# First batch of a banded attention and feed-forward kernel: band windows of v loaded first, the feed-forward cut at f = 4 and 9, other staging places for the weights

## The chip, the cores and the metric

The kernel runs on one core of a Trainium2 chip. The metric is the device time of one execution in microseconds (us), as the median of several runs. The engines are TensorE (PE, with its weight loads PEld), VectorE (DVE), ScalarE (ACT), GpSimd (POOL) and SyncE (SP). In this kernel SP only issues the transfers.

## The reference, cut to what matters

```python
# q, k, v: (8 batches, 8 heads, 576 positions, 64)
q_d, k_d, v_d = mean over 4 neighbouring positions          # 144 positions
out_up    = repeat(softmax(q_d k_d^T / 8) v_d, 4)            # the pooled part
out_local = softmax(q k^T / 8 where |i - j| < 4) v           # the banded part
x   = out_up + out_local, as (8 * 576 tokens, 512)
h   = x @ w_in                                               # (512, 2048)
out = max(0.01 * h, h) @ w_out                               # (2048, 512)
```

Everything is float32. The weights are float64 in memory (two 32-bit words per number).

## The kernel before, in words

**The feed-forward (called MoE in the names).** A half of a batch is a tile of 256 tokens (hf = 0) or 320 tokens (hf = 1). The hidden dimension is cut into 16 blocks f of 128. One step (half, f) is 12 matmuls of the up projection (L638), two activations and a subtraction (`leaky`, L648 to L651), and 12 matmuls of the down projection (L678) into four accumulators, the PSUM banks `acc0` to `acc3`. Each float32 product is made of three matmuls, on a high and a low part: `xh`, `xl` of x, `wih`, `wil`, `woh`, `wol` of the weights, `gh`, `gl` of the activation. `PASSES` lists the halves with their range of f. For batch 0 each half is done in two ranges, f 0 to 7 and f 8 to 15, in the order (0,0) low, (0,1) low, (0,0) high, (0,1) high. What a first range leaves is stored to the output (`store`, ACT copy at L713), loaded again (`refetch`) and added to the second range (DVE, L704). The other batches take all 16 blocks at once.

**The weights.** `convert(f, k)` brings one tile of w_in (k = 0) or w_out (k = 1): it takes a staging place, loads 512 KB, and makes the high and low parts with ACT (L226, L231, L239), DVE (L228, L233) and POOL (L241). There are 32 such tiles. The staging place is a buffer of another stage: `k`, `v`, the two `prod`, `up`, and for f below 4 also `xh1` and `xl1`. It is held until the POOL instruction at L241 is done. For f of 9 and above there is room for the result only when the pool `su` is closed (signal `late`), after all pooled and banded work of batch 0.

**Batch 0.** For each pair of heads c (four of them), `pooled(0, c)` makes the pooled attention (scores L312, softmax with ACT L324, transposes L351, values L363). `banded(0, c, hf)` makes the banded part with small matmuls: a mask and scores (L405, L413), the softmax (DVE L420, L421, L426, L430, ACT L424, L428, POOL L432), transposes (L440) that ACT copies into `su_pt` (L442), then the values (L458) from `su_pt` and the band windows of v, `su_vw`, and at last the sum with the pooled part and the split into `xh` and `xl` (L470, L475, L477). `su_pt` has two buffers, so two (c, hf) are under way at a time. `su_vw` has four. The load of a window is asked for only after the transposes, inside `banded`. The second half waits until all four c of the first half have their x.

**The other batches.** `scores` and `values` make the band with POOL products (L507, L562) and DVE sums (L513, L568), `widen` spreads the pooled part into `up`, `landing` transposes and adds (L598, L605, L611, L613). `pooled` needs `qk` and `vs`, one buffer each.

**The order.** All of it is written by a planner (`Order`): each task is a generator with a rank; the next instruction is the one that can start first by the planner's costs, and among equal ones that of the lowest rank. The engines, and SP with its transfers, then run their instructions strictly in the planned order. Buffers are granted to the waiting task of the lowest rank.

Of the kernel before, what the change touches and what calls it, by code (L numbers as in the profile page):

```python
# [6 lines left out]
F32 = mybir.dt.float32  # L7
# [25 lines left out]
WORDS = 2  # L33
REBIAS = 2.0 ** -112
LOW, ROUND = 0.876 * 2.0 ** -29, 0.484375
HF = NF // 2
PASSES = ([((0, 0), 0, HF), ((0, 1), 0, HF), ((0, 0), HF, NF), ((0, 1), HF, NF)]
# [107 lines left out]
def attn_moe(ctx: ExitStack, tc, qkt, vd, qb, kb, vb0, vb1, vwb, band, identb, w_in, w_out, ident, edge, out):  # L145
# [8 lines left out]
                xloc=2, lst=3, lvw=1, gh=3, gl=3, o=4, hp=2, pt=2, xh0=1, xl0=1, xh1=1, xl1=1, acc0=1, acc1=1, acc2=1, acc3=1,  # L154
                su_vw=NC, su_pt=2)
# [20 lines left out]
    def pe(us, *after):  # L176
        return (yield ("op", "PE", us, max(after) + SAFE, 0))
# [38 lines left out]
    def convert(f, k):  # L216
        s = yield from slot("k", "v", "prod", "up", *(("xh1", "xl1") if f < 4 else ()))
# [38 lines left out]
    def x_tile(b, hf):  # L256
        if b:
            yield from wait(("xbuf", b - 1, hf))
        elif hf:
            yield from wait(("x", 0, 0), NC)  # L260
# [4 lines left out]
        t = yield from wait(("done", b, hf), 2 if b == 0 else 1)  # L265
# [3 lines left out]
    def fetch(b, c, pool):  # L269
# [3 lines left out]
        else:  # L273
            sq = sv = None
            qk = pool.tile([128, 2, S], F32, name=f"qk{c}")
            vs = pool.tile([72, 2, 2, D, FAC], F32, name=f"vs{c}")
# [96 lines left out]

    shared, wide = {}, {}
# [4 lines left out]
    def banded(b, c, hf, rank, pool=None):  # L379
# [7 lines left out]
        if b:  # L387
            yield from wait("late")
        elif hf:
            yield from wait(("x", 0, 0), 4)  # L390
# [10 lines left out]
        s_b = yield from slot("hp" if (b, hf) == (0, 0) else "pt")  # L401
# [43 lines left out]
        if b:  # L445
            yield from wait(("pooled", b, NC - 1))
            yield from wait(("xbuf", b, hf))
        s_vw = yield from (slot("su_vw") if b == 0 else slot("q", "lvw"))
        vw = sb(s_vw, [WIN, 5, 2, D], F32, pool)
        tv = yield from load(vw[:, :nb], vwb[b, c, :, b0:b1], 35840 * nb, s_vw.t)  # L450
# [125 lines left out]
    def widen(b, hf, u):  # L576
        to = yield from wait(("pooled", b, 2 * u))
        to = max(to, (yield from wait(("pooled", b, 2 * u + 1))))
        tx = yield from wait(("xbuf", b, hf))
        s_u = yield from slot("up")  # L580
# [41 lines left out]
    def up_proj():  # L622
        for i, (p, f) in enumerate(steps):
# [3 lines left out]
            if f == f0:  # L627
                tx = yield from wait(("x", b, hf), 4)
            tw = yield from wait(("w", f, 0))
# [26 lines left out]
    def down_proj():  # L656
        for i, (p, f) in enumerate(steps):
# [5 lines left out]
            if f == f0 + 2 and f0 > 0:  # L663
# [26 lines left out]
    def refetch(p, e, n):  # L690
        s_o = yield from slot("o")
        o = sb(s_o, [128, 320], F32)
        tw = yield from wait(("half", PASSES[p][0]), 4)
# [4 lines left out]
    def store(p, e, n, s_a, acc, t):  # L698
# [18 lines left out]
        if f1 < NF:  # L717
            od.signal(("half", key), t)
# [11 lines left out]
    with tc.manual_schedule():  # L730
# [5 lines left out]
        for c in range(NC):  # L736
            od.spawn(1 + c, pooled(0, c, 1 + c, sup))
            od.spawn(1.5 + c, banded(0, c, 0, 1.5 + c, sup))
            od.spawn(26 + 0.1 * c, banded(0, c, 1, 26, sup))
        for f in range(NF):  # L740
            for k in range(2):
                od.spawn((20 if f < HF else 40) + 2 * (f % HF) + k, convert(f, k))
# [74 lines left out]
```

## Time and profile before

| | |
|---|---|
| median of 3 runs | 985.31 us (983.8 to 986.4) |
| profiled execution | 980.87 us, span 979.1 us, mean granted clock 0.983 |
| PE busy, matmuls | 948.0 us (97%), 7434 |
| DVE busy | 616.5 us (63%) |
| ACT busy | 432.2 us (44%) |
| POOL busy | 613.5 us (63%) |
| moved by DMA | 106.46 MB, mean 109 GB/s |

Busy time is a sum over the whole span. Matmuls are pipelined, so their single durations overlap. In a timeline row the columns are start, duration, engine, line, operation, output and inputs, shape, count, and in brackets the idle time before it with what ended it. In a row by windows the columns are the window, its length, the busy time of each engine with its count of instructions, the granted TensorE clock, the share of DMA time and GB/s.

### The profile page before, as it was taken

To read this page: it belongs to the slowest core of one execution; us is meant where nothing else is said; L and a number is where in the kernel's file an instruction comes from. 1 tells how busy PE (TensorE), PEld (TensorE's weight loads), DVE (VectorE), ACT (ScalarE), POOL (GpSimd) and SP (SyncE) were. 2 spreads that over 40 slices of the span, in tenths; PEclk is the share of its full clock that TensorE was granted. 3 is DMA by queue.
4 is the path that set the end of the run, shared out by engine and by line. 5 is a ranking of instruction groups with operands and counts; after the bars stand their busy time and mean duration, and the time that the engine had idled before them with its cause. 6 is when DMAs were issued, how large, how long until landed. Compare 5 with 4: busy or idle time off the path is not lost.

```text
span 979.1 us, 18709 instructions
## 1 busy us (share of the span) xinstructions
PE 948.0 (97%) x7434; PEld 913.0 (93%) x7434; DVE 616.5 (63%) x987; ACT 432.2 (44%) x1251; POOL 613.5 (63%) x362
## 2 busy tenths in 40 slices
PE   5796999999999999999999999999999999999998
PEld 4596999889999999999999999999999999999998
DVE  4997778878866877587665976547563756151111
ACT  4887966444533543255422554234332324242212
POOL 3553467888797878887787878758695777310000
PEclk9597999999999999999999999999999999999999
DMA  9546763624531542225223441304131121000000
GB/s 286 188 148 204 232 223 127 197 99 156 166 108 56 185 136 94 68 92 179 82 89 109 154 147 61 111 4 158 39 108 55 54 71 52 30 23 6 23 1 27
DMA packets 51959, 106.46 MB, mean 109 GB/s; under 512 B 4464, under 2 KB 30320, under 8 KB 51872
## 3 DMA queue, kind: packets, MB, share of 16 engines
q1 hardware_dynamic: 51872, 105.28, 32.9%
q8 instruction: 58, 0.95, 0.4%
q14 instruction: 29, 0.24, 0.1%
HBM read 94.64 MB, written 10.62 MB: 108 GB/s over the span
## 4 chain that ended last, share of the span: by engine, by line
PE 91%; DMA 3%; ACT 2%; issue 1%; DVE 1%; POOL 1%; SPq 0%; POOLq 0%; ACTq 0%
PE hp L638 42%; PE acc L678 40%; PE pt L312 2%; PE pt L363 2%; PE pt L351 2%; DMA su_vw<-in_vwb_dram 1%; PE pt L598 1%; DMA v<-in_w_out_dram 1%; DMA vs<-in_vd_dram 1%; POOL wol L241 0%; POOL wil L241 0%; DVE prod L228 0%; PE pt L413 0%; ACT pd L324 0%; SPq L181 0%
## 5 line engine op out<-in xcount | busy, mean ns | idle before, releaser
L562 POOL TENSOR_TENSOR prod<-v,s 128x896 f32<-128x896 f32 (+1 forms) x112 | 270.1, 2417 | 85.8 <-DVE xloc L568 64.3
L638 PE MATMUL hp<-xh,wih 128*128 128x320 f32 (+1 forms) x1024 | 312.7, 305 | 1.7 <-ACT xh L611 1.3
L678 PE MATMUL acc<-gh,woh 128*128 128x320 f32 (+1 forms) x1024 | 307.9, 301 | 0.5 <-ACT o L713 0.4
L638 PE MATMUL hp<-xl,wih 128*128 128x320 f32 (+1 forms) x1024 | 304.0, 297 | 0.1
L638 PE MATMUL hp<-xh,wil 128*128 128x320 f32 (+1 forms) x1024 | 303.8, 297 | 0.0
L678 PE MATMUL acc<-gh,wol 128*128 128x320 f32 (+1 forms) x1024 | 301.8, 295 | 0.0
L678 PE MATMUL acc<-gl,woh 128*128 128x320 f32 (+1 forms) x1024 | 301.7, 295 | 0.0
L507 POOL TENSOR_TENSOR prod<-q,k 128x896 f32<-128x896 f32 (+1 forms) x112 | 265.1, 2373 | 36.1 <-DMA k<-in_kb_dram 22.9
L648 ACT ACTIVATE gh<-hp 128x320 fp32r<-128x320 f32 (+1 forms) x256 | 105.4, 412 | 364.5 <-PE acc L678 339.6
L651 DVE TENSOR_TENSOR gl<-hp,gh 128x320 fp32r<-128x320 f32 (+1 forms) x256 | 116.2, 455 | 221.4 <-ACT hp L649 220.3
L638 PEld LDWEIGHTS hp<-xh,wih 128*128 128x128 f32 x1024 | 194.6, 190 | 8.6 <-issue 5.5
L678 PEld LDWEIGHTS acc<-gh,woh 128*128 128x128 f32 x1024 | 192.7, 188 | 4.7 <-issue 2.6
L638 PEld LDWEIGHTS hp<-xl,wih 128*128 128x128 f32 x1024 | 195.0, 190 | 0.3 <-DVE xl L613 0.3
L638 PEld LDWEIGHTS hp<-xh,wil 128*128 128x128 f32 x1024 | 194.8, 190 | 0.0
L678 PEld LDWEIGHTS acc<-gl,woh 128*128 128x128 f32 x1024 | 192.7, 188 | 0.0
L678 PEld LDWEIGHTS acc<-gh,wol 128*128 128x128 f32 x1024 | 192.4, 188 | 0.0
L568 DVE TENSOR_REDUCE xloc<-prod 128x128 f32<-128x896 f32 (+1 forms) x112 | 133.9, 1196 | 22.7 <-POOL prod L562 21.4
L513 DVE TENSOR_REDUCE s<-prod 128x14 f32<-128x896 f32 (+1 forms) x112 | 133.4, 1193 | 19.5 <-POOL prod L507 19.1
L649 ACT ACTIVATE hp<-hp 128x320 f32<-128x320 f32 (+1 forms) x256 | 104.0, 406 | 0.0
L605 DVE TENSOR_TENSOR pt<-pt,up 128x256 f32<-128x256 f32 (+1 forms) x56 | 38.7, 709 | 32.3 <-PE pt L598 30.6
L299 DVE TENSOR_REDUCE qk_d<-qk 128x288 f32<-128x1152 f32 x29 | 38.9, 1342 | 11.8 <-DMA qk<-in_qkt_dram 11.7
L324 ACT ACTIVATE pd<-pt,st_d 128x144 f32<-128x144 f32 x84 | 32.0, 381 | 26.8 <-DVE st_d L321 19.5
(119 smaller groups left out, 777.5 us busy)
## 6 DMA issues: line engine op xcount, KB each, us to landing
qk<-in_qkt_dram SPq DMA_DIRECT2D x32, 576.0 KB
k<-in_kb_dram SPq DMA_DIRECT2D x14, 704.0 KB
v<-in_vb_dram SPq DMA_DIRECT2D x14, 704.0 KB
vs<-in_vd_dram SPq DMA_DIRECT2D x32, 288.0 KB
k<-in_kb_dram SPq DMA_DIRECT2D x14, 640.0 KB
v<-in_vb_dram SPq DMA_DIRECT2D x14, 640.0 KB
out_dram<-o SPq DMA_DIRECT2D x36, 160.0 KB
out_dram<-o SPq DMA_DIRECT2D x36, 128.0 KB
```

The source lines that it names most:

```text
L299: nc.vector.tensor_reduce(out=qk_d, in_=qkr, axis=AX.X, op=ALU.add)
L324: nc.scalar.activation(out=pd[:, qi], in_=scv[:, qi], func=AF.Exp, scale=SCALE / (FAC * FAC), bias=mx[:, qi:qi + 1], accum_out=sm[:, qi:qi ...
L507: nc.gpsimd.tensor_tensor(out=prv, in0=q[:, p, a - j0:z - j0].unsqueeze(2).to_broadcast([128, n, W, D]), in1=view(k[:, p], (a - j0) * D, [ ...
L513: nc.vector.tensor_reduce(out=s[:, p, a - j0:z - j0], in_=prv, axis=AX.X, op=ALU.add)
L562: nc.gpsimd.tensor_tensor(out=prv, in0=view(v[:, p], a - j0, [[1, n], [nv, D], [1, W]]), in1=s[:, p, a - j0:z - j0].unsqueeze(2).to_broadc ...
L568: nc.vector.tensor_reduce(out=xl_t[:, :n, p], in_=prv, axis=AX.X, op=ALU.add)
L605: nc.vector.tensor_tensor(out=xv, in0=xv, in1=upv, op=ALU.add)
L638: nc.tensor.matmul(hp[:, :n], wt[:, c], x[:, c], start=k == 0, stop=k == 3 * NC - 1)
L648: nc.scalar.activation(out=gh[:, :n], in_=hp[:, :n], func=AF.Prelu, alpha=0.01)
L649: nc.scalar.activation(out=hp[:, :n], in_=hp[:, :n], func=AF.Prelu, alpha=0.01)
L651: nc.vector.tensor_tensor(out=gl[:, :n], in0=hp[:, :n], in1=gh[:, :n].bitcast(F32), op=ALU.subtract)
L678: nc.tensor.matmul(acc[:, :n], wt[:, es], g[:, :n], start=f == f0 and j == 0, stop=f == f1 - 1 and j == 2)
```

## The change

- `PASSES`: batch 0 is done in three ranges of f, cut at 4 and 9, each range for both halves. So there are two more passes that store what they have, and two more that load it again. `refetch` is asked for one step earlier and waits for the pass two before it.
- The windows of v get tasks of their own (`windows`), with ranks from 1.2 to 8.2. The first half's windows have their four `su_vw` buffers and are no longer asked for after the transposes; the second half's windows use the four buffers of `vs` of batch 0 (`su_vs`) after these have been summed.
- The second half of `banded(0)` and its `xh1`, `xl1` wait for the scores of c = 3 of the first half, not for the whole x; its rank is 21, not 26.
- The score bank of the first half is `acc{(c + 2) % 4}`, not `hp`.
- Staging places: `v`, `up`, `vs` and a new buffer `stg` for all f, in addition `k` and the two `prod` for f below 8, and `xh1`, `xl1` for f below 4. The ranks of `convert` follow f alone.
- The planner's cost of small PE groups rises by 0.09 us; `widen` takes `up` in a fixed order.

```diff
+OWN = 8
-HF = NF // 2
-PASSES = ([((0, 0), 0, HF), ((0, 1), 0, HF), ((0, 0), HF, NF), ((0, 1), HF, NF)]
+CUTS = (0, 4, 9, NF)
+PASSES = ([((0, hf), f0, f1) for f0, f1 in zip(CUTS, CUTS[1:]) for hf in range(2)]
           + [((b, hf), 0, NF) for b in range(1, B) for hf in range(2)])
...
-                xloc=2, lst=3, lvw=1, gh=3, gl=3, o=4, hp=2, pt=2, xh0=1, xl0=1, xh1=1, xl1=1, acc0=1, acc1=1, acc2=1, acc3=1,
-                su_vw=NC, su_pt=2)
+                xloc=2, lst=3, stg=1, gh=3, gl=3, o=4, hp=2, pt=2, xh0=1, xl0=1, xh1=1, xl1=1, acc0=1, acc1=1, acc2=1, acc3=1,
+                su_vw=NC, su_vs=NC, su_pt=2)
...
-        return (yield ("op", "PE", us, max(after) + SAFE, 0))
+        return (yield ("op", "PE", us + 0.09, max(after) + SAFE, 0))
...
     def convert(f, k):
-        s = yield from slot("k", "v", "prod", "up", *(("xh1", "xl1") if f < 4 else ()))
+        s = yield from slot("v", "up", "vs", "stg", *(("k", "prod") if f < OWN else ()), *(("xh1", "xl1") if f < 4 else ()))
...
     def x_tile(b, hf):
...
         elif hf:
-            yield from wait(("x", 0, 0), NC)
+            yield from wait(("scored", 0, NC - 1))
...
-        t = yield from wait(("done", b, hf), 2 if b == 0 else 1)
+        t = yield from wait(("done", b, hf), len(CUTS) - 1 if b == 0 else 1)
...
     def fetch(b, c, pool):
...
-            sq = sv = None
+            sq, sv = None, (yield from slot("su_vs"))
             qk = pool.tile([128, 2, S], F32, name=f"qk{c}")
-            vs = pool.tile([72, 2, 2, D, FAC], F32, name=f"vs{c}")
+            vs = sb(sv, [72, 2, 2, D, FAC], F32, pool)
...
+    vws = {}
+
+    def windows(c, hf, pool):
+        b0, b1 = BLKS[hf]
+        s_vw = yield from slot("su_vs" if hf else "su_vw")
+        vws[c, hf] = s_vw, sb(s_vw, [WIN, 5, 2, D], F32, pool)
+        t = yield from load(vws[c, hf][1][:, :b1 - b0], vwb[0, c, :, b0:b1], 35840 * (b1 - b0), s_vw.t)
+        od.signal(("vw", c, hf), t)
...
     def banded(b, c, hf, rank, pool=None):
...
         elif hf:
-            yield from wait(("x", 0, 0), 4)
+            yield from wait(("scored", 0, NC - 1))
...
-        s_b = yield from slot("hp" if (b, hf) == (0, 0) else "pt")
+        s_b = yield from slot(f"acc{(c + 2) % NC}" if (b, hf) == (0, 0) else "pt")
...
-        if b:
-            yield from wait(("pooled", b, NC - 1))
-            yield from wait(("xbuf", b, hf))
-        s_vw = yield from (slot("su_vw") if b == 0 else slot("q", "lvw"))
-        vw = sb(s_vw, [WIN, 5, 2, D], F32, pool)
-        tv = yield from load(vw[:, :nb], vwb[b, c, :, b0:b1], 35840 * nb, s_vw.t)
+        tv = yield from wait(("vw", c, hf))
+        s_vw, vw = vws[c, hf]
...
     def widen(b, hf, u):
...
+        if (b, hf, u) != (BANDED, 0, 0):
+            yield from wait(("up", *((b, hf, 0) if u else (b, 0, 1) if hf else (b - 1, 1, 1))))
         s_u = yield from slot("up")
...
-            if f == f0 + 2 and f0 > 0:
+            if f == f0 + 1 and f0 > 0:
...
-        tw = yield from wait(("half", PASSES[p][0]), 4)
+        tw = yield from wait(("half", p - 2), 4)
...
-            od.signal(("half", key), t)
+            od.signal(("half", p), t)
...
-            od.spawn(26 + 0.1 * c, banded(0, c, 1, 26, sup))
+            od.spawn(21 + 0.1 * c, banded(0, c, 1, 21, sup))
+            for hf in range(2):
+                od.spawn(1.2 + c + 4 * hf, windows(c, hf, sup))
...
-                od.spawn((20 if f < HF else 40) + 2 * (f % HF) + k, convert(f, k))
+                od.spawn(20 + 2 * f + k, convert(f, k))
```

More of the change, by code (lines that the diff above doesn't have):

```diff
@@ L628, in up_proj @@
                 tx = yield from wait(("x", b, hf), 4)
+                od.signal("started")
             tw = yield from wait(("w", f, 0))
```

## The prediction

> **What bounds the kernel now.** I read the page first, then the span by windows, the chain of waits, and the timelines of PE, ACT, DVE, POOL and SP over the first 200 us.
>
> ```profile
> PE   5796999999999999999999999999999999999998
> PEclk9597999999999999999999999999999999999999
> ```
> ```profile
> 0.00:48.50 48.50, 32.36 (x295) 22.37 (x295) 34.14 (x62) 32.28 (x86) 21.10 (x25) 0.80 0.78 239
> 48.50:77.50 29.00, 28.79 (x291) 27.29 (x289) 26.98 (x52) 25.07 (x64) 15.29 (x12) 0.99 0.52 167
> 77.50:92.90 15.40, 7.67 (x86) 5.89 (x84) 11.45 (x18) 10.59 (x28) 4.05 (x4) 0.80 0.77 243
> 92.90:193.10 100.20, 99.81 (x769) 93.99 (x770) 79.67 (x127) 66.79 (x188) 66.67 (x41) 0.98 0.57 180
> 193.10:199.30 6.20, 3.05 (x26) 2.22 (x25) 5.49 (x14) 3.41 (x13) 2.83 (x2) 1.00 1.02 374
> 199.30:979.10 779.80, 776.27 (x5977) 761.22 (x5977) 458.75 (x718) 294.05 (x876) 503.59 (x280) 1.00 0.25 84
> ```
>
> The page's 40 slices show PE full from the ninth on, so the kernel is PE-bound for 780 of its 979 us and only the first 200 us have anything to give. The windows (first busy time: PE, third: DVE) cut these at the events of PE. To 48.5 us there is no MoE step. To 77.5 us half (0,0) runs f 0 to 7 with PE full: the weights come fast enough. To 92.9 us PE has no MoE step, since x of half (0,1) isn't there. Then it is full to 193.1 us, waits 6.2 us for x of half (1,0), and never again.
>
> ```profile
> 85.51 3.93 DMA su_vw<-in_vwb_dram
> 92.90 4.26 PE hp L638 x15
> 116.64 3.96 PE acc L678 x27
> 199.29 5.24 PE hp L638 x29
> 213.08 2.87 PE hp L638 x24
> ```
>
> These rows of the chain (start, duration, what) give the prices: 0.12 us per matmul of 256 tokens (213.08), 0.147 of 320 (116.64), so a step of 24 costs 2.87 or 3.5 us. They also show that a wait is paid twice: after the wait to 92.9 us 15 matmuls take 4.26 us instead of 2.2, after that to 199.3 us 29 take 5.24 instead of 3.5.
>
> **The change part by part.**
>
> *Windows ahead.* Why is x(0,1) ready only at 93 us?
>
> ```profile
> 16.48 1.28 SPq L181 DMA_DIRECT2D su_vw<-in_vwb_dram  x1
> 73.37 0.38 SPq L181 DMA_DIRECT2D su_vw<-in_vwb_dram  x1
> 133.23 4.53 SPq L181 DMA_DIRECT2D out_dram<-o  x3
> ```
> ```profile
> 19.77 0.24 ACT L442 COPY su_pt<-pt 70x128 f32<-70x128 f32 x1
> 24.23 0.26 ACT L442 COPY su_pt<-pt 70x128 f32<-70x128 f32 x1
> 41.70 0.64 ACT L442 COPY su_pt<-pt 70x384 f32<-70x384 f32 x2 [0.17 <-PE pt L440]
> 59.91 0.37 ACT L442 COPY su_pt<-pt 70x256 f32<-70x256 f32 x1
> ```
> ```profile
> 27.75 0.69 PE L458 MATMUL acc<-su_pt,su_vw 70*64 70x64 f32 x16
> 28.37 0.29 PE L405 MATMUL hp<-band_sb,idb_sb 128*128 128x280 bf16 x1
> 33.00 1.12 PE L458 MATMUL acc<-su_pt,su_vw 70*64 70x64 f32 x16
> 34.06 0.41 PE L405 MATMUL hp<-band_sb,idb_sb 128*128 128x280 bf16 x1
> 43.91 1.12 PE L458 MATMUL acc<-su_pt,su_vw 70*64 70x64 f32 x16 [0.98 <-DMA su_vw<-in_vwb_dram]
> 46.72 0.47 PE L405 MATMUL pt<-band_sb,idb_sb 128*128 128x350 bf16 x1
> 64.80 0.80 PE L458 MATMUL pt<-su_pt,su_vw 70*64 70x64 f32 x20
> 69.47 0.32 PE L405 MATMUL pt<-band_sb,idb_sb 128*128 128x350 bf16 x1
> 89.58 1.34 PE L458 MATMUL pt<-su_pt,su_vw 70*64 70x64 f32 x20 [3.71 <-DMA su_vw<-in_vwb_dram]
> ```
>
> The weights of c = 0 lie ready at 20.0 us (ACT, 19.77 + 0.24), those of c = 1 at 24.5. The value matmuls (L458) run at 27.75 and 33.0 us, because the windows go out behind weight tiles in SP's queue (16.48 us the first). The next scores (L405) need the `su_pt` that these matmuls give back, and follow 0.6 to 4.7 us later (28.37, 69.47). So eight heads' halves go through two buffers in four rounds, and each late window delays the rest.
>
> With the windows ahead, L458 of c = 0 and 1 come at 20.3 and 24.8 us. The scores of c = 2 and 3 don't follow at once: their bank is now `acc0` or `acc1`, which c = 0 and 1 hold from L458 until the split (L477):
>
> ```profile
> 32.16 0.41 DVE L477 TENSOR_TENSOR xl<-acc,xh 128x256 fp32r<-128x256 f32 x1
> 37.32 0.41 DVE L477 TENSOR_TENSOR xl<-acc,xh 128x256 fp32r<-128x256 f32 x1
> 93.13 0.49 DVE L477 TENSOR_TENSOR xl<-pt,xh 128x320 fp32r<-128x320 f32 x1 [0.82 <-ACT xh L475]
> ```
>
> That is 4.8 and 4.7 us, so the scores start at 25.1 and 29.5 us, 3.3 and 4.6 us earlier than 28.37 and 34.06. The last L458 of the first half moves by 4.6 us from 43.91 to 39.3, and MoE starts at about 44 us instead of 48.5. The second half's c = 1 starts its scores at 46.72 - 4.6, about 42.5 with the four windows (0.57 MB) that now pass ahead of the weights.
>
> From there two rounds remain, c = 1 and then c = 3. From scores to the last copy a round took 8.3 us at the least (34.06 to 42.34) and 13.6 at the most (46.72 to 60.28), on a DVE that was busy 27.0 of 29.0 us. I take 11: four steps of `leaky` fewer and no pooled work of batch 1 lie beside it now, but the conversions still do. Between rounds 0.6 to 4.7 us, I take 2.6; L458 to the split 4.0 (89.58 to 93.62). x(0,1) comes at 42.5 + 11 + 2.6 + 11 + 4.0 = 71 us; I use 72. With all the low ends it is 63, with all the high ends 79.
>
> *Three ranges.* After f 0 to 3 of (0,0), 4 x 2.87 = 11.5 us, PE needs x(0,1), where before it had 23 us of MoE. With MoE at 44 us and some 6 us of banded matmuls among it, PE is through at 61 to 62 us and then waits for x(0,1), with a few us of banded work inside. So the cut moves f 4 to 7 of (0,0), 11.5 us, behind x(0,1). What the early x(0,1) brings is 92.9 - 72 = 20.9 us, of which 11.5 goes back here.
>
> The pooled matmuls of batch 1 that filled the old wait move behind it too, which I put at 3.5 us of the 7.67 in that window. Two more borders between passes cost a wait for an accumulator:
>
> ```profile
> PE acc L678 <- ACT o L713: 0.4, 1, 0.4
> ```
>
> 0.4 us each, 0.8 in all; between 0 and 0.8, I take the high end. The eight further stores and eight reloads move 2.3 MB, hidden where DMA is 57% busy. On SP a store that waits for its copy holds up what is queued behind it (133.23: three in 4.53 us), here weight tiles; two more such blocks cost 0 to 9 us of SP, nothing on PE while the weights are ahead. The eight further additions (L704) lie on DVE, at 80% there.
>
> *The weights.*
>
> ```profile
> 49.05 1.32 POOL L241 TENSOR_TENSOR wol<-k,woh 128x512 fp32r<-128x512 f32 x1 [1.32 <-ACT woh L239]
> 95.41 1.31 POOL L241 TENSOR_TENSOR wil<-v,wih 128x512 fp32r<-128x512 f32 x1 [10.17 <-ACT wih L239]
> 134.16 1.32 POOL L241 TENSOR_TENSOR wol<-up,woh 128x512 fp32r<-128x512 f32 x1 [0.29 <-ACT woh L239]
> ```
>
> f 3 was complete at 50.4 us; now f 4 is needed only at 72 + 14 = 86 us and f 9 at about 118. From 95.41 to 134.16, 14 tiles passed through five places, 2.8 us each, so a place was held 14 us. f 8 to 15 now have four places for 16 tiles: four rounds, 56 us. They start near 63 us, as before, and end near 119. Hidden, with some 15 us of slack on the last f.
>
> *Batch 1.* `k` and `prod` are free after f 7, near 80 us, so POOL's products start long before 131 us. But `vs` is a staging place now, and pooled(1, 0) waits until conversions let it go, at about 112 us.
>
> ```profile
> 129.97 1.34 DVE L299 TENSOR_REDUCE qk_d<-qk 128x288 f32<-128x1152 f32 x1
> 160.34 1.34 DVE L299 TENSOR_REDUCE qk_d<-qk 128x288 f32<-128x1152 f32 x1
> ```
>
> Four heads of batch 2 were 10.1 us apart (three steps from 129.97 to 160.34). Load 6, three steps 30, the last head through in 17, landing 4: x(1,0) at 169 us at the earliest.
>
> *The sum.* From x(0,1) PE has the 100.2 us of the fourth window, 11.5 + 3.5 + 0.8 us: MoE of batch 0 ends at 72 + 116 = 188 us. x(1,0) is there, so of the fifth window only its 3.05 us of work stays, and of the last 779.8 us the slow clock behind the wait goes, 5.24 - 3.5 = 1.7 us. The end is 188 + 3 + 778.1 = 969.1 us, 10.0 below the span of 979.1. The profiled execution took 980.87 us, 4.4 below the median of 985.31. Taken off the median it gives 975 us.
>
> **The rivals.**
>
> *No wait at (0,1).* If rounds take 8.3 us, x(0,1) comes at 63 us, just as PE is through with f 3. Nine us more are saved: 966. For it speaks the smaller load on DVE, against it that only one round was so short.
>
> *Batch 1 is late (slower).* The mechanism is `vs` under conversions. If a place is held 21 us, not 14, the last tiles end at 63 + 84 = 147 us, pooled(1, 0) starts about 140, and x(1,0) comes at 197: the 10 us are gone. From there each us of holding costs 4; at 23 us PE starts batch 1 some 8 us later than that: 993. Against it speaks 14 us by the rows; for it, that the first tiles now meet banded work of both halves.
>
> *The windows don't decide.* If DVE is the limit of every round (27 of 29 us busy), rounds take 13.6 us and the early start is all there is: x(0,1) at 79 us, 7 of the 10 us lost: 982.
>
> *POOL beside the conversions.*
>
> ```profile
> 41.23 1.78 DVE L233 SCALAR_TENSOR_TENSOR xh<-xh 128x512 int32<-128x512 int32 x1
> 42.93 0.68 DVE L228 SCALAR_TENSOR_TENSOR k<-k 128x512 int32<-128x512 int32 x1
> ```
>
> A DVE pass over a weight tile took 0.68 us, or up to 1.78 where a POOL instruction ran. The products of batch 1 now fall among the conversions of f 8 to 15: 32 passes, up to 1.1 us more each, 35 us of DVE at the most, about 18 at half overlap. DVE had 20 us idle in the fourth window, so x(1,0) and the last weights would slip into PE's path by some 5 us: 980. The Trainium skill ("Advanced Engine Details and Errata", VectorE Performance Modes) says that GpSimd and two-port VectorE instructions share an SBUF port and block each other; the two rows agree with it. By that rule in full the gain would shrink, by the short passes alone it would not.
>
> **How the numbers follow.** Forecast 0.48 (970 to 979), no wait 0.16 (966), windows don't decide 0.14 (982), late batch 1 0.14 (985 to 995), POOL 0.08 (980). The time is 975 us. The range 964 to 987 leaves out the worse part of the late batch and the best of "no wait". About 0.3%, 3 us, is what a measurement can tell from no change. Faster by more: 0.48 + 0.16 + 0.06 + 0.04 = 0.74. Slower by more: 0.12. The rest, 0.14, lies between.
>
> **What would show it.** The windows' transfers leave SP before 10 us; L458 of c = 0 near 20 us; the first L638 near 44; a hole without L638 from about 62 to 72, then rows of 320 columns; no hole at the start of batch 1, near 190 us; 16 additions at L704, where two passes of four made 8. Wrong if the hole ends after 80 us, if L638 waits for `wil`, or if the first product of batch 1 meets a hole near 190 us because L299 of batch 1 comes later than about 140.

## The result, and the profile after

The changed kernel took 995.21 us (median of 4 runs, 993.18 to 997.96) against 985.1 of the kernel before: a ratio of 1.011, 95% interval 1.0093 to 1.0128. It is slower by about 1.1%. The prediction was 975 us, faster. Its profiled execution took 993.18 us with a span of 991.4, where that of the kernel before had 979.1. One run of an experiment below (`w_pool`) took 5152.67 us and is left out of that kernel's ratio.

The line numbers of the changed kernel are a few higher: up projection L647 (before L638), down projection L687 (L678), scores of the band L415 and L423 (L405, L413), values L464 (L458), split L483 (L477), weight passes of DVE L229 and L234 (L228, L233), POOL's last step of a tile L242 (L241), products L513 (L507), pooling sum L300 (L299), subtraction of `leaky` L660 (L651).

From the page of the changed kernel, the slices of PE and of the granted clock:

```profile
PE   5887999999999999999999999999999999999998
PEclk9597999999999999999999999999999999999999
```

At this coarseness it is the page before. The windows between the events of PE tell more: the first step of half (0,1), of half (1,0) and of half (2,0). First the kernel before, then the changed one (columns as before: PE, PEld, DVE, ACT, POOL, clock, DMA, GB/s):

```profile
0.00:92.83 92.83, 68.75 (x666) 55.48 (x667) 72.57 (x130) 67.87 (x176) 40.45 (x40) 0.86 0.70 217
92.83:196.57 103.74, 101.58 (x787) 95.33 (x785) 82.74 (x135) 68.19 (x194) 66.77 (x42) 0.98 0.59 187
196.57:311.83 115.26, 113.88 (x880) 110.09 (x879) 86.76 (x134) 51.02 (x158) 97.14 (x53) 0.99 0.33 110
311.83:979.10 667.27, 663.74 (x5108) 652.08 (x5106) 374.42 (x590) 245.11 (x724) 409.18 (x229) 1.00 0.24 81
```
```profile
0.00:77.76 77.76, 56.27 (x532) 43.66 (x532) 59.16 (x105) 54.34 (x139) 39.51 (x38) 0.78 0.73 213
77.76:193.16 115.40, 108.20 (x805) 102.65 (x803) 103.03 (x149) 70.59 (x182) 88.92 (x54) 0.96 0.62 199
193.16:321.93 128.77, 125.07 (x1008) 116.63 (x1005) 105.34 (x171) 65.84 (x215) 105.76 (x59) 1.00 0.44 142
321.93:991.40 669.47, 663.63 (x5099) 651.89 (x5096) 361.43 (x573) 242.20 (x717) 386.30 (x213) 1.00 0.23 76
```

From the last event on both have the same work of PE before them, and need about the same time (667 and 669 us). The 10.1 us are lost before it. Half (0,1) does begin earlier, at 77.8 us, and half (1,0) by 3.4 us. But PE idles 7.2 us between these two where it idled 2.2, and (1,0) to (2,0) takes 13.5 us more, with 128 more PE instructions in it: pooled work of later batches that the kernel before had behind it by then.

Because the two kernels do the work in another order, I count the time that PE lost up to a moment: the time since the start of the span, minus what the matmuls finished by then cost at full rate (0.1195 us for 256 columns and 0.1465 for 320, from long undisturbed stretches; the small ones likewise). All kernels here have the same 7434 matmuls, so at the end these times differ just as the spans do. At the earlier moments they are good to some 2 us, since they depend on the rate taken for the small matmuls. In us:

| lost up to | 50 us | 90 us | 200 us | the end |
|---|---|---|---|---|
| before | 30.4 | 38.4 | 47.6 | 51.3 |
| changed | 29.9 | 46.2 | 53.3 | 63.6 |

The difference at the end, 12.3, is the difference of the spans. From 50 to 90 us the changed kernel loses 16.3 us instead of 8.0. From 90 to 200 us it loses 7.1 instead of 9.2. Behind 200 us it loses 10.3 instead of 3.7, so a good half of the difference arises only there.

**The first loss, seen in the timelines.** PE, from 19 to 84 us (the rows that the steps of the prediction name, and one wait):

```profile
19.70 0.69 PE L464 MATMUL acc<-su_pt,su_vw 70*64 70x64 f32 x16
23.34 0.43 PE L450 MATMUL pt<-id_sb,xloc 128*70 128x128 f32 x1 [2.96 <-ACT su_pt L452]
27.07 1.07 PE L464 MATMUL acc<-su_pt,su_vw 70*64 70x64 f32 x16
28.72 0.44 PE L415 MATMUL acc<-band_sb,idb_sb 128*128 128x280 bf16 x1
44.98 0.47 PE L415 MATMUL pt<-band_sb,idb_sb 128*128 128x350 bf16 x1
60.29 0.80 PE L464 MATMUL pt<-su_pt,su_vs 70*64 70x64 f32 x20
63.75 0.32 PE L415 MATMUL pt<-band_sb,idb_sb 128*128 128x350 bf16 x1 [1.05 <-DVE xloc L431]
76.50 1.34 PE L464 MATMUL pt<-su_pt,su_vs 70*64 70x64 f32 x20 [1.13 <-DVE xl L483]
83.61 0.63 PE L647 MATMUL hp<-xh,wih 128*128 128x320 f32 x1 [3.08 <-ACT xh L481]
```

c = 0 has its values at 19.7 us as forecast, without waiting for a window. c = 1 has them only at 27.1 us. Its copy into `su_pt` (L452), for which PE waits 2.96 us, stood on ACT behind a pass over the first weight tile, which lands 3 us later now that some 1 MB of windows goes ahead of it or among the weights:

```profile
22.27 0.65 ACT L227 ACTIVATE v<-v 128x512 int32<-128x512 uint32 x1 [3.83 <-DMA v<-in_w_in_dram]
```

The same pass of the kernel before ran at 19.20. Then the second half: c = 1 takes 15.3 us from scores to values, c = 3 takes 12.8, and from its values to its split 7.6 us pass. In these rounds each small instruction takes its place in a queue with conversions. The scores of c = 1 were done at 46.8 us, but the first step of its softmax (L430) stands on DVE behind a weight pass:

```profile
46.87 1.45 DVE L229 SCALAR_TENSOR_TENSOR xh<-xh 128x512 int32<-128x512 int32 x1
48.24 0.51 DVE L430 TENSOR_REDUCE lst<-pt 128x5 f32<-128x350 f32 x1
```

The rows of DVE and POOL behind the values of c = 3 show what holds its split up:

```profile
77.67 1.79 DVE L229 SCALAR_TENSOR_TENSOR vs<-vs 128x512 int32<-128x512 int32 x1
79.38 2.58 DVE L229 SCALAR_TENSOR_TENSOR stg<-stg 128x512 int32<-128x512 int32 x1
81.88 0.68 DVE L234 SCALAR_TENSOR_TENSOR up<-up 128x512 int32<-128x512 int32 x1
82.48 0.49 DVE L476 TENSOR_TENSOR pt<-pt,outd 128x320 f32<-128x320 f32 x1
83.59 0.49 DVE L483 TENSOR_TENSOR xl<-pt,xh 128x320 fp32r<-128x320 f32 x1
```
```profile
78.88 2.53 POOL L513 TENSOR_TENSOR prod<-q,k 128x896 f32<-128x896 f32 x1
```

DVE runs its instructions in the planned order, and three passes over weight tiles stand before the sum at L476. A product of batch 1 has begun on POOL, the only one before 84 us, and beside it a pass that takes 0.68 us elsewhere takes 2.58. x(0,1) is complete at 84.1 us. The hole is where the prediction put it, but longer: the up projection (L647) stops at 59.1 us, the down projection of f 0 to 3 lasts until 69.1, and but for nine matmuls from 77.8 us on, the up projection goes on only at 83.6.

**Behind it.** The pooling of batch 1 begins at

```profile
134.86 1.34 DVE L300 TENSOR_REDUCE qk_d<-qk 128x288 f32<-128x1152 f32 x1
```

where the kernel before had its four sums at 60, 83, 98 and 112 us. Apart from the 3.08 us above, PE's waits from 83 us to the start of half (2,0) are short ones, for a DVE that was busy 95.5 of the 108 us from 92 to 200 (85.7 in the kernel before). The numbers are us in total, waits, and the longest:

```profile
PE hp L647 <- DVE gl L660: 6.1, 9, 1.8
```

### The profile page after: what moved, and what is told of

It is laid out like the page before. It is cut to its first block, busy times and chain, and to the rows that moved or that the text cites. A ratio compares the mean times of both kernels' runs of the same rounds, so it can differ in the third digit from the quotient of the medians.

```text
span 991.4 us, 18736 instructions
## 1 busy us (share of the span) xinstructions
PE 953.2 (96%) x7434; PEld 914.8 (92%) x7434; DVE 629.0 (63%) x995; ACT 433.0 (44%) x1251; POOL 620.5 (63%) x362
## 4 chain that ended last, share of the span: by engine, by line
PE 76%; POOL 7%; DMA 6%; DVE 5%; issue 3%; ACT 2%; SPq 1%; POOLq 0%; DVEq 0%; ACTq 0%
PE hp L647 35%; PE acc L687 34%; POOL prod L513 3%; PE pt L352 2%; PE pt L313 2%; POOL prod L568 2%; DMA qk<-in_qkt_dram 2%; PE pt L364 2%; DMA v<-in_vb_dram 1%; POOL wil L242 1%; PE pt L606 1%; DMA v<-in_w_in_dram 1%; POOL wol L242 1%; DMA su_vs<-in_vd_dram 1%; DVE s L519 1%
## 5 line engine op out<-in xcount | busy, mean ns | idle before, releaser
L647 PE MATMUL hp<-xh,wih 128*128 128x320 f32 (+1 forms) x1024 | 314.4, 307 | 10.6 <-DVE gl L660 7.3
L687 PE MATMUL acc<-gh,woh 128*128 128x320 f32 (+1 forms) x1024 | 307.0, 300 | 0.8 <-ACT o L722 0.7
L647 PE MATMUL hp<-xl,wih 128*128 128x320 f32 (+1 forms) x1024 | 304.3, 297 | 0.0
L647 PE MATMUL hp<-xh,wil 128*128 128x320 f32 (+1 forms) x1024 | 303.7, 297 | 0.0
L687 PE MATMUL acc<-gl,woh 128*128 128x320 f32 (+1 forms) x1024 | 301.7, 295 | 0.0
L687 PE MATMUL acc<-gh,wol 128*128 128x320 f32 (+1 forms) x1024 | 301.7, 295 | 0.0
L513 POOL TENSOR_TENSOR prod<-q,k 128x896 f32<-128x896 f32 (+1 forms) x112 | 266.1, 2383 | 26.5 <-DMA k<-in_kb_dram 16.2
L660 DVE TENSOR_TENSOR gl<-hp,gh 128x320 fp32r<-128x320 f32 (+1 forms) x256 | 115.7, 453 | 228.6 <-ACT hp L658 228.2
L647 PEld LDWEIGHTS hp<-xh,wih 128*128 128x128 f32 x1024 | 195.0, 190 | 19.0 <-DVE gl L660 10.9
L687 PEld LDWEIGHTS acc<-gh,woh 128*128 128x128 f32 x1024 | 192.7, 188 | 4.6 <-issue 2.4
L647 PEld LDWEIGHTS hp<-xl,wih 128*128 128x128 f32 x1024 | 195.2, 191 | 0.2 <-DVE xl L483 0.2
L647 PEld LDWEIGHTS hp<-xh,wil 128*128 128x128 f32 x1024 | 195.1, 191 | 0.0
L687 PEld LDWEIGHTS acc<-gl,woh 128*128 128x128 f32 x1024 | 192.7, 188 | 0.1
L687 PEld LDWEIGHTS acc<-gh,wol 128*128 128x128 f32 x1024 | 192.4, 188 | 0.0
L519 DVE TENSOR_REDUCE s<-prod 128x14 f32<-128x896 f32 (+1 forms) x112 | 133.5, 1192 | 18.5 <-POOL prod L513 18.1
L325 ACT ACTIVATE pd<-pt,st_d 128x144 f32<-128x144 f32 x84 | 32.0, 381 | 42.5 <-DVE st_d L322 37.7
L300 DVE TENSOR_REDUCE qk_d<-qk 128x288 f32<-128x1152 f32 x29 | 39.0, 1346 | 14.8 <-DMA qk<-in_qkt_dram 14.5
```

What stands on the lines that cost most here:

```text
L300: nc.vector.tensor_reduce(out=qk_d, in_=qkr, axis=AX.X, op=ALU.add)
L325: nc.scalar.activation(out=pd[:, qi], in_=scv[:, qi], func=AF.Exp, scale=SCALE / (FAC * FAC), bias=mx[:, qi:qi + 1], accum_out=sm[:, qi:qi ...
L513: nc.gpsimd.tensor_tensor(out=prv, in0=q[:, p, a - j0:z - j0].unsqueeze(2).to_broadcast([128, n, W, D]), in1=view(k[:, p], (a - j0) * D, [ ...
L519: nc.vector.tensor_reduce(out=s[:, p, a - j0:z - j0], in_=prv, axis=AX.X, op=ALU.add)
L647: nc.tensor.matmul(hp[:, :n], wt[:, c], x[:, c], start=k == 0, stop=k == 3 * NC - 1)
L660: nc.vector.tensor_tensor(out=gl[:, :n], in0=hp[:, :n], in1=gh[:, :n].bitcast(F32), op=ALU.subtract)
```

## The experiments

Nineteen kernels are compared with the kernel before, which ran beside each on the same chip. Ratios have their 95% intervals; below 1 is faster.

| kernel | ratio | lost up to 50 / 90 / 200 / end, us |
|---|---|---|
| changed | 1.0110 (1.0093 to 1.0128) | 29.9 / 46.2 / 53.3 / 63.6 |
| w_only: windows alone | 0.9957 (0.9935 to 0.9979) | 23.4 / 33.0 / 43.6 / 48.5 |
| c_only: three ranges alone | 1.0054 (1.0034 to 1.0074) | 31.0 / 49.5 / 55.1 / 60.8 |
| s_only: staging alone | 1.0084 (1.0054 to 1.0115) | 30.2 / 40.7 / 54.8 / 59.5 |
| b_pe: planner's 0.09 us alone | 1.0037 (1.0022 to 1.0052) | 31.4 / 39.5 / 50.4 / 54.4 |
| a_two: changed, two ranges | 1.0027 (1.0004 to 1.0049) | 29.6 / 34.8 / 48.6 / 53.0 |
| a_hold: changed, scores held | 1.0069 (1.0049 to 1.0088) | 30.2 / 44.1 / 56.2 / 61.4 |
| a_novs: changed, other staging | 1.0088 (1.0059 to 1.0117) | 29.9 / 47.7 / 58.8 / 66.7 |
| a_hp: changed, bank hp | 1.0025 (1.0009 to 1.0041) | 29.4 / 49.5 / 55.3 / 59.4 |
| a_pe0: changed, without 0.09 us | 1.0126 (1.0088 to 1.0163) | 31.5 / 49.4 / 58.1 / 68.5 |
| a_nod: changed, one DVE pass less | 0.9992 (0.9974 to 1.0010) | 28.7 / 42.8 / 47.4 / 52.1 |
| b_nod: before, one DVE pass less | 1.0025 (1.0007 to 1.0043) | 31.6 / 35.6 / 46.4 / 55.2 |
| a_pt: changed, four su_pt | 1.0086 (1.0056 to 1.0115) | 28.7 / 39.3 / 53.1 / 61.2 |
| a_pt_novs: the same, without vs | 1.0109 (1.0085 to 1.0134) | 31.3 / 43.8 / 52.6 / 65.3 |
| w_stg: windows and stg | 1.0023 (1.0007 to 1.0039) | 28.0 / 38.4 / 51.7 / 58.3 |
| w_pool: windows, pooling of batch 1 on POOL | 1.0038 (1.0023 to 1.0053) | 27.5 / 34.4 / 50.1 / 57.2 |
| w_pe9: windows, 0.09 us | 1.0016 (0.9997 to 1.0034) | 26.6 / 35.6 / 47.9 / 56.1 |
| w_pt: windows, four su_pt | 0.9952 (0.9931 to 0.9973) | 27.9 / 34.7 / 48.6 / 51.0 |
| w_pt_novs: the same, other staging | 1.0067 (1.0045 to 1.0090) | 25.8 / 35.4 / 52.8 / 61.5 |

The kernel before has 30.4 / 38.4 / 47.6 / 51.3. The lost time is that of the one profiled execution. A kernel's own runs spread by some 3 us and more, so it need not follow the ratio exactly (the profiled run of a_hp was the slowest of its runs, 988.97 us).

### One part alone: windows, ranges

w_only takes `windows`, `su_vs` and the waits for them from the change and leaves the rest as before.

```diff
+            for hf in range(2):
+                od.spawn(1.2 + c + 4 * hf, windows(c, hf, sup))
...
+        tv = yield from wait(("vw", c, hf))
+        s_vw, vw = vws[c, hf]
```

> The kernel before with only the windows moved ahead of the weights (their own tasks, second half in the vs buffers of batch 0). Theory C (the three ranges ask for x(0,1) before it can be there, and that eats what the windows bring): the waits for windows in front of L458 (1.0, 1.6 and 3.7 us of PE in the profile before) go and x(0,1) comes some 8 us earlier, so about 977 us. Theory P (the change loses by POOL products of batch 1 among the conversions) and theory V (it loses by vs as a staging place) expect the same 977, since neither is in this kernel. Rival W (the windows in front delay the first weight tile by 3 us, and that costs as much as they bring): 984 to 988.

Measured 979.97 us. MoE starts at 41.7 us instead of 48.5, x(0,1) is complete at 82.0 instead of 93.6. Half (1,0) starts at 189 us instead of 197, and PE waits for it: 10.0 us are lost between 160 and 200 us, where the kernel before lost 4.2. The gain is half of what was expected, though x(0,1) came 11.6 us earlier and not 8. W's forecast fell: the later weight tile doesn't eat it.

c_only has the cuts, their reloads and the ranks of the conversions, and nothing else.

```diff
+CUTS = (0, 4, 9, NF)
+PASSES = ([((0, hf), f0, f1) for f0, f1 in zip(CUTS, CUTS[1:]) for hf in range(2)]
```

> The kernel before with only the three ranges of f (cut at 4 and 9, with the reloads that they need). Theory C: x(0,1) still comes near 92 us, PE has 11.5 us of MoE less in front of it, the hole at 77 to 93 us becomes one from about 62: some 10 us slower, 994 to 997. Theories P and V: the ranges cost only two borders, 985 to 988.

Measured 990.45 us, 5 us slower than before and less than C's 10. In the profile the loss has C's place and size. x(0,1) is complete at 90.7 us (93.6 before), PE is through with f 0 to 3 by 64, and from 50 to 90 us it loses 18.5 us instead of 8.0. The windows of that kernel, with PE first and the clock third from the end:

```profile
49.30:61.00 11.70, 11.70 (x92) 11.57 (x91) 11.14 (x23) 9.55 (x24) 5.52 (x5) 0.91 0.39 122
61.00:87.30 26.30, 13.41 (x166) 10.13 (x164) 23.40 (x36) 20.86 (x49) 14.54 (x11) 0.64 0.65 205
```

PE is idle for 13 us of the second window, and the mean granted clock over it is 0.64. Some of the loss comes back from 90 to 200 us (5.6 us lost instead of 9.2).

### Undoing one part of the change: ranges, products among the conversions

a_two sets `CUTS = (0, 8, NF)` in the changed kernel and asks for `refetch` where the kernel before does.

> The changed kernel with two ranges of f, cut at 8, as before. Theory C: (0,0) runs 8 steps, 23 us from 49.5, and covers the wait for x(0,1) at 84 us to within some 10 us, so the 11.5 us come back: 981 to 985. Theories P and V: the ranges are not the cause, 991 to 996.

Measured 986.28 us: 8.3 of the changed kernel's 10.9 us are gone (ratio 1.0027 for 1.0110). The loss from 50 to 90 us falls from 16.3 to 5.2. With c_only this bears theory C out from both sides: at the time of the hole, the 11.5 us of MoE that the cut moved were the cover. It isn't the cover alone, as x(0,1) is complete at 79.2 us here, 4.9 us sooner, and c_only is the cleaner test. Not all returns, since 13.8 us are lost from 90 to 200 us where the changed kernel lost 7.1: half (1,0) starts at 186.3 us, only 7 us sooner.

a_hold keeps the products of the other batches back until the last weight tile is done.

```diff
         yield from wait("ready")
+        yield from wait(("w", NF - 1, 1))
```

> The changed kernel with the scores of the other batches held until the last weight tile is converted, so that POOL has no product (L513) among the conversions. Theory P: the DVE passes over weight tiles go back to a mean below 1 us, x(0,1) comes 2 to 4 us earlier than 84, the short waits for L660 up to 140 us go: 986 to 990. Theory V: pooled(1) is as late as it was, and the products now are later too: 996 to 1005. Theory C: 994 to 997.

Measured 990.81 us, 4 us faster than the changed kernel, just above the range of P. The 64 passes L229 and L234 take 61.2 us in sum where the changed kernel takes 71.8 and the kernel before 57.4. x(0,1) is complete at 81.0 us instead of 84.1. The forecasts of V (996 or more) and of C (994 to 997) fell. P is seen in the passes. In the time it isn't shown: 0.41% is little more than the 0.37% that a new plan alone moves (b_pe below).

### Staging places, the bank, the windows with one more place

s_only has the new staging places and the fixed order of `widen`.

```diff
+        s = yield from slot("v", "up", "vs", "stg", *(("k", "prod") if f < OWN else ()), *(("xh1", "xl1") if f < 4 else ()))
```

> The kernel before with only the staging places changed (v, up, vs and stg for all f, k and prod below f = 8), and widen taking up in its fixed order. Theory V (vs as a staging place makes pooled(1) late, and its PE and DVE work falls into batch 1): the first L299 of batch 1 comes after 110 us instead of 60, slower by 3 to 8 us, 987 to 992. Theory P (what hurts is POOL's products beside the conversions, which start when k and prod are free): the first product moves from 131 to about 85 us, the DVE passes grow to a mean of 1.1 us, 987 to 990. Theory C (the ranges alone): no change, 983 to 985.

Measured 991.58 us, the worst of the single parts. The first product moves from 131 to 75 us, the passes over the tiles take 74.7 us in sum, and the first pooling sum of batch 1 moves from 60 to

```profile
134.43 1.35 DVE L300 TENSOR_REDUCE qk_d<-qk 128x288 f32<-128x1152 f32 x1 [1.40 <-DMA qk<-in_qkt_dram]
```

P and V both forecast these places in the trace, and the kernel doesn't part them; the time lies in V's range and just above P's, and C's forecast of no change fell. a_novs should part them, and puts `"v", "up", "stg", "k", "prod"` for all f into the changed kernel:

> The changed kernel with the staging places v, up, stg, k and prod for all f, so that vs is left to pooled and k and prod are not free early. Theory V: pooled(1) starts before 100 us again, and of the 10 us that the change lost against before some 5 to 7 come back, 986 to 989. Theory P alone: like the kernel with the scores held back, 990 to 991, since the products start late again. Theory C: 990 or more.

Measured 992.24 us. Pooling of batch 1 begins early again, the products late, and the passes are short (58.0 us in sum):

```profile
96.23 1.34 DVE L300 TENSOR_REDUCE qk_d<-qk 128x288 f32<-128x1152 f32 x1
```

Yet half (1,0) starts at 201 us and the kernel is by the ratios only 2 us faster than the changed one, within the intervals of both. V alone falls as the cause. With a_hold: early products with late pooling, late products with early pooling, and both late come to 1.0110, 1.0088 and 1.0069.

a_hp takes the first half's score bank from `hp` again.

> The changed kernel with the score bank of the first half taken from hp, as before. Theory K (the accumulator banks, which c = 0 and 1 hold until their split, keep the scores of c = 2 and 3 back): x(0,0) is complete at 42 us instead of 49.7 as in the kernel with the windows alone, x(0,1) follows some 5 us earlier, near 79, and the time falls by 3 to 6 us, 988 to 991. If x(0,1) stays at 84, K holds for MoE's start and not for the time: 994.

Measured 986.26 us, 8.5 us less than the changed kernel, below both forecasts, but not by K. x(0,0) is complete at 49.5 us, no earlier, and x(0,1) at 88.5, later. What went is the loss behind 200 us: 4.1 us instead of 10.3. This one edit takes back most of the slowdown, with a larger loss before 90 us than in the changed kernel. Its engines' queues are in another order from the start, and I can't name a mechanism by which the bank does this.

w_stg gives the windows alone one more staging place:

> The kernel before with the windows ahead and one more staging place (stg, for all f), and nothing else of the change. Theories V and C: neither vs nor the ranges are touched, so it stays below before, 976 to 981; the additional place can only bring the weights earlier. Theory P: more conversions meet in one stretch, DVE is the limit there, x(0,1) doesn't come earlier than the 82 us of the kernel with the windows alone: 979 to 982.

Measured 986.05 us: x(0,1) at 89.8 us, half (1,0) at 194. One more place with no other edit made it 0.7% slower. All three theories had expected less than before.

### Is DVE the limit, and how much is the plan

a_nod and b_nod leave out the first DVE pass over each weight tile, in the changed kernel and in the kernel before.

```diff
-        t1 = yield from op("DVE", 870, t)
-        nc.vector.scalar_tensor_tensor(out=li, in0=ti, scalar=-(1 << 31), in1=li,
-                                       op0=ALU.bitwise_and, op1=ALU.bitwise_or)
-        t = yield from op("ACT", 512, t1)
+        t = yield from op("ACT", 512, t)
```

> The changed kernel without the first DVE pass over each weight tile (L229, which merges the sign into the low word); so it computes with other weights, and DVE has 32 instructions less, 36 us at their mean of 1.12. Theory D (in the first 200 us DVE is the limit, and decides both when x(0,1) and when x(1,0) come, so that ranges and windows only move the hole): x(0,1) before 76 us instead of 84, x(1,0) before 175 instead of 193, the time falls by 12 us or more, to 983 or below. Rival O (the fixed order of the queues and the two su_pt buffers decide, DVE is full only because there is time): x(0,1) stays above 80, the time above 990.

> The kernel before without the same pass (L228). Theory D: batch 1 is no longer late, x(0,1) still waits for its windows; 974 to 980, and the changed kernel without the pass comes out level with it or better, since its order pays once DVE has room. Rival O: 983 to 986, no change, and the changed kernel stays slower by 8 us or more.

Measured 982.74 and 986.54 us. The changed kernel gains 12 us, as D had it. But x(0,1) came at 79.0 us, not before 76, and half (1,0) starts at 184.6, not before 175. The kernel before gained nothing: it got slower by 2.5 us with 32 instructions less. There MoE starts at 54.0 us instead of 48.5, in another order of the queues. D holds in part for the changed kernel and not for the other. O, which had the changed kernel above 990 us, falls for that one; for the kernel before it comes near, with 986.5 for 983 to 986.

b_pe is the test of that: the kernel before with 0.09 us more in the planner's cost, the same work.

> The kernel before with only the planner's cost of small PE groups raised by 0.09 us: the same work, planned anew. Theory N (a new plan by itself moves the time by some us, because every queue is in another order): more than 3 us away from 984, to either side. Otherwise 982 to 986.

Measured 987.02 us, 3.6 above its comparison by the ratio: a new plan alone is worth 0.37% here (MoE at 52.7 us, x(0,1) at 98.4). Differences of that size between two plans, whatever the edit, are no evidence on the edit.

a_pe0 and w_pe9 repeat the change and the windows under the other value of that cost:

> The changed kernel with the planner's cost of small PE groups as it was before (without the 0.09 us). Theory N (a new plan alone moves the time by some 4 us): anything from 988 to 998, the loss against before remains at least at 4 us, since the hole before x(0,1) and the late pooled(1) are not of the plan's making. If it falls to 984 or below, the whole loss was a chance of one plan.

> The kernel before with the windows ahead, and the 0.09 us added: the windows under another plan. Before with the 0.09 us took 987.0. If the windows are worth something by themselves, x(0,0) is complete near 42 us again and the time lies 3 to 6 us below that, 981 to 984. Theory N: the 4 us that they brought were a chance of the plan, 985 to 988.

a_pe0 took 997.16 us, so the loss is no chance of one plan. w_pe9 took 985.75, against 987.02 of b_pe with the same cost: MoE starts at 43.8 us and x(0,0) is complete at 43.5, where b_pe has 52.7 and 53.4. The windows' mechanism holds in the trace. The time lies in the range of theory N: under that plan the windows bring 0.2%, with intervals that overlap (1.0016, 0.9997 to 1.0034; 1.0037, 1.0022 to 1.0052).

w_pool moves the pooling sum of batch 1 from DVE to POOL in w_only:

> The kernel before with the windows ahead, and the pooling of q and k of batch 1 made by two POOL additions (as for batch 0) in place of the DVE sum at L299: 4 x 1.34 us less on DVE, 4 x 1.85 more on POOL, between 60 and 130 us. Theory D: x(1,0) comes 3 to 6 us earlier, 975 to 978. Rival O: as the windows alone, 979 to 981, or slower, as POOL waits too.

Measured 988.38 us. The four sums of batch 1 were finished by POOL additions at 37, 97, 115 and 134 us, where w_only had them on DVE at 84, 105, 124 and 133. So the pooling was not later, and yet half (1,0) starts at 201 us instead of 189. D's forecast fell, and what held batch 1 up is not shown.

### What sets x(0,1), and where its gain goes

a_pt and w_pt have four `su_pt` and three `xloc`, in the changed kernel and in w_only.

```diff
-                xloc=2, lst=3, ...
-                su_vw=NC, su_vs=NC, su_pt=2)
+                xloc=3, lst=3, ...
+                su_vw=NC, su_vs=NC, su_pt=4)
```

> The changed kernel with four su_pt buffers and three xloc, so that three (c, hf) can be under way, not two. Theory R (two buffers make four rounds of 11 to 15 us, and these set x(0,1)): x(0,1) comes near 72 us instead of 84, of the 16 us that PE loses between 50 and 90 us 6 to 10 come back, 985 to 989. Theory D (DVE sets it): x(0,1) stays at 80 or later, 993 to 996.

> The kernel before with the windows ahead and four su_pt buffers and three xloc. Theory R: the second half's scores start as soon as its x may, x(0,1) comes near 74 us instead of 82, 974 to 978. Theory D: 979 to 983, the hole moves to the start of batch 1, whose x comes at 189 us whatever is done before.

In a_pt x(0,1) is complete at 74.0 us (its last split):

```profile
73.51 0.49 DVE L483 TENSOR_TENSOR xl<-pt,xh 128x320 fp32r<-128x320 f32 x1
```

R had it near 72, and D at 80 or later. DVE was nearly as full there (37.1 of the 40 us from 50 to 90). Up to 160 us PE has lost 43.9 us there, 8.1 less than in the changed kernel. But the time is 993.62 us, in D's range. Half (1,0) starts at 191 us, and 9.2 us are lost between 160 and 200 us where the changed kernel lost 1.3. PE waits there for the late pooling:

```profile
188.89 1.71 PE L313 MATMUL pt<-qk_d 64*64 64x144 f32 x12 [3.89 <-DVE qk_d L300]
```

So in the changed kernel the number of buffers sets x(0,1) (`su_pt` or `xloc`, which are not parted here), and what more of them give is given back at the start of batch 1. In w_pt R's forecast fell: x(0,1) came at 80.2 us, not near 74, against 82.0 in w_only. There the second half still waits for the whole x of the first. w_pt is the fastest kernel of the study, 0.9952 (0.9931 to 0.9973), level with w_only; both are faster than the changed kernel, and than the kernel before by a little more than what a new plan alone moves. The 13.3 us that w_pt loses between 160 and 200 us point to the start of batch 1 once more.

The last two free both roads to batch 1: `vs` is no staging place, and `k` and `prod` are free behind f 7.

```diff
+        s = yield from slot("v", "up", "stg", *(("k", "prod") if f < 8 else ()), *(("xh1", "xl1") if f < 4 else ()))
```

> The changed kernel with four su_pt and three xloc, and without vs as a staging place: v, up, stg for all f, k and prod below f = 8. In every kernel so far x of half (1,0) let PE start batch 1 between 184 and 201 us. Theory G (of the two roads to it one is always late: pooled(1) where vs is a staging place, the products where k and prod are): with both free early it starts before 180 us, the 9 us that PE lost between 160 and 200 us in the kernel with four su_pt are at most 4, and the time is 980 to 986. Theory D (DVE and POOL are simply full until then): it starts at 188 us or later, 990 or more. Three places for the last 16 tiles may bring the last weights after 145 us, which would show as waits of PE for wil or wol.

> The kernel before with the windows ahead, four su_pt and three xloc, and the same staging places (v, up, stg for all f, k and prod below 8; widen in its fixed order), in two ranges. Theory G: batch 1 starts before 182 us instead of 192, and of the 13 us that PE lost between 160 and 200 us half come back: 972 to 976. Theory D: 979 to 984, the start of batch 1 stays at 188 us or later.

995.18 and 991.12 us: G falls, and the second time is above D's range (979 to 984) as well. Pooling begins at 81 us, the products at 78, and half (1,0) starts at 202 and 201 us all the same. But the last weight tile is done only at 167 and 171 us (137 in the changed kernel), so three places were too few, and the test doesn't tell a full DVE (96.9 of 108 us busy from 92 to 200 us in a_pt_novs) from late weights. Why batch 1 never started before 184 us stays open.

## Why the prediction was wrong, by its own steps

The forecast was a span 10.0 us shorter, and it came out 12.3 longer, 22.3 us apart. By the table of lost time this gap falls into three parts. Up to 90 us the changed kernel lost 7.8 us more, where the sum had 5.1 less (20.9 gained, 11.5 + 3.5 + 0.8 given back): 12.9 us. From 90 to 200 us it lost 2.1 less, where the sum had 4.9 less at the start of batch 1: 2.8 us. Behind 200 us it lost 6.6 more, where the sum had nothing.

**What bounds the kernel.** Right in part: the holes of the first 200 us are where the windows showed them. The loss behind 200 us, 6.6 us more than before, was in no step. It goes with pooled work that came late (128 more PE instructions between the starts of (1,0) and (2,0)) and with short waits for DVE. a_hp and a_two don't have it, with the same staging, so staging alone doesn't make it, and what decides it is open.

**Windows ahead.** L458 of c = 0 at 20.3 us: right (19.7). c = 1 at 24.8: 27.1, since ACT stood idle 3.8 us for the first weight tile. I had looked only at who waits for the windows, not at what waits behind the tile that they push back. Scores of c = 2 came at 28.7 us for 25.1, MoE at 49.5 for 44. The bank, which I had charged with 4.8 us, is not shown to be the cause: with `hp` back, MoE started at 48.1.

**x(0,1) at 72 us: the step that failed.** It came at 84.1. The start of c = 1's scores was 2.5 us late (44.98 for 42.5), the two rounds took 15.3 and 12.8 us from scores to values for 11 and 11 (14.3 and 13.2 to the last copy, where I had 13.6 at the most), between them 3.5 for 2.6, and values to split 7.6 for 4.0: 13 us over the 71 of that sum (12 over the 72 that I used), nearly the whole of the 12.9 us above. I had taken DVE for relieved. It was busy 38.1 of the 40 us from 50 to 90, where the kernel before had 35.7, with longer passes over the weights. The upper end that I had given, 79, left out that the last split can stand behind conversions. That the buffers make the rounds was right for the changed kernel (a_pt: 74.0 us).

**Three ranges.** The 11.5 us were right in size: c_only lost 10.5 us more in the hole, and a_two got 11.1 back, part of it by an earlier x(0,1). The error was to set them against a gain of 20.9 us. That gain was 9.5 (93.6 to 84.1), and with it the sum turns: 11.5 to pay, 9.5 to pay with.

**The weights and batch 1.** The 14 us that a place is held were right only for the later rounds: of the tiles from f = 8 on, the first three, asked for from 62 to 67 us, held theirs for 22 to 23 us, and the fourth place came free only at 79. The other 13 tiles held theirs for 12 to 17 us, 14.3 in the mean. So the last tile was done at 137 us, not 119, the first pooling sum came at 135, not 118, and half (1,0) started at 193, not 169. These places in the trace lie near those of the rival "batch 1 is late" (147, 140, 197). By that rival's own sum a start at 193 would have meant some 981 us, so it is luck that 995 falls at the upper end of its 985 to 995. PE had no long wait there, since MoE of batch 0 itself ended at about 193 us and not at 188.

**POOL beside the conversions.** This rival happened too, in part. The passes took 14.4 us more (71.8 for 57.4), for which I had put 18. But only 9.5 of it stand beside seven products, most of the rest beside POOL's own steps of the conversion, and only one product began before x(0,1) was complete. a_hold brought back 4 us of the time, hardly more than a new plan does. The rival was given a chance of 0.08 as one of five cases; in truth it came together with the long rounds and the late batch 1, and the range was made from cases that exclude one another.

**The clock.** It went down in the hole as it had in the wait before 92.9 us. PE was busy 1.96 of the 5.2 us from 69.0 to 74.2, at a granted clock of 1.00, and from 74.3 to 87.9 us the clock was granted at 0.50. The Trainium skill ("TensorE: Matmul & The Clock Gate", What's actually happening) has the clock at half after an idle window of about 3.4 us. The trace agrees on the half. It doesn't show the window: from 69.0 us until the clock fell, no idle stretch of PE was longer than 1.7 us.

## What to carry to other kernels

Before a pipeline is cut finer so that a second stage can begin earlier, ask what its first part was covering: here the cut took 11.5 us of cover from a wait that became only 9.5 us shorter. Price the arrival of such a stage from the rows of the loaded engine, with what stands in its in-order queue at the last step. Where a planner writes the order of every queue, run it once with a harmless change of its costs: here that alone moved the time by 0.37%, so single plans say nothing about gains of that size or smaller, and part-by-part comparisons need the place in the trace beside the ratio.

## What the runs showed of the hardware that I had not expected

A DVE pass over a weight tile (128x512, two SBUF inputs) that takes 0.68 us alone took 2.58 us beside a POOL product of 2.53 us. I had taken 1.78 for the most, from its runs beside the shorter POOL step of a conversion (1.3 us alone). In the rows above the product ends at 81.41 us and the pass at 81.96, 0.55 us later. A pass beside a conversion step ends as long behind it:

```profile
74.06 1.44 POOL L242 TENSOR_TENSOR wol<-prod,woh 128x512 fp32r<-128x512 f32 x1 [0.27 <-ACT woh L240]
74.26 1.78 DVE L234 SCALAR_TENSOR_TENSOR v<-v 128x512 int32<-128x512 int32 x1
```

So does every pass of the two kernels that began while a POOL instruction ran and took longer than 0.73 us: it ended 0.55 to 0.58 us behind that instruction. In sum the 64 passes were 57.4 us with few products beside them and 71.8 with many. The Trainium skill ("Advanced Engine Details and Errata", VectorE Performance Modes) says that GpSimd and two-port VectorE instructions block each other. Whether this pass is such an instruction no run here shows; that it is blocked the rows do show, and that the delay goes up with what is left of POOL's instruction.
